# A gated dilated convolution on one Trainium2 core: matmuls reordered around waits, a load held back, a warm-up on a constant

## The chip, the core and the metric

The kernel runs on one core of a Trainium2 chip. The core has engines that work side by side, each through its own list of instructions in order: TensorE (matmuls; PE in the profile, with its weight loads as PEld), VectorE (DVE), ScalarE (ACT), GpSimd (POOL) and SyncE (SP), which here issues nearly all DMAs. They wait for one another by semaphores. Operands lie in SBUF, and matmul results in PSUM, whose banks hold 128 x 512 float32 each. The metric is device time in microseconds (us), the median of several runs.

## The reference

The input x has 2 sequences of 16000 steps with 256 channels, in bfloat16. A causal convolution with three taps at distance 2 makes 512 channels; the first half goes through tanh, the second through a sigmoid, the two are multiplied, and a 256 x 256 matrix projects the product.

```python
pad = (K - 1) * dil                      # K = 3, dil = 2
xp = jnp.pad(x, ((0, 0), (pad, 0), (0, 0)))
h = jnp.einsum('btc,cd->btd', xp[:, pad:pad + T, :], w[0])
for i in range(1, K):
    off = pad - i * dil
    h = h + jnp.einsum('btc,cd->btd', xp[:, off:off + T, :], w[i])
f = h[..., :D].copy()
g = h[..., D:].copy()
z = jnp.tanh(f) * _sigmoid(g)
return z @ w_o
```

## The kernel before

**Tiling.** The 32000 steps are cut into group 0 (512 steps), an extra group (512), an end group (256) and 15 wide groups of 2048. x is brought in with channels on partitions by transposing DMAs from SP (`load_plain` for the extra group, tile `xte`; `load_wide`, tile `xq`, two buffers; `load_end`, tile `xe`). Group 0 alone is loaded plainly (tile `osb`) and transposed on TensorE. Each group has four blocks, one for 128 of the 512 convolution channels, in the order tanh, sigmoid, tanh, sigmoid. Blocks are numbered through: 0 to 3 are group 0, 4 to 7 the first wide group, 8 to 11 the second, up to 63. The extra and end groups have blocks of their own.

**A wide block** does not apply the three taps one by one. VectorE first makes sums and differences of x at eight phases (tiles `q`, `qp`, `qm`, `qd`: `wide_pairs` L213, `wide_p` L219, `wide_m` L222, `wide_d` L231; GpSimd does quarters of `qd`). With weights combined at the start (`wmh`, `wph`, `wm`, `wt`, `wu`, `wd0`, `wd2`), TensorE then runs 14 matmuls of 512 columns into one two-bank PSUM tile `y` (three buffers):

- `first`, two with `wmh` on `qp` (L254); ScalarE copies the bank to `st` (`keep_first`, L276);
- `second`, two with `wph` on `qm` (L246); ScalarE copies the bank to `sv` (L280), and GpSimd makes the second half of `sv` (`other`, L283);
- `third`, two with `wm` on the other half of `qm`; then VectorE's `split_bank` (L286) forms the second bank of `y`;
- `late(0)`, four with `wt` and `wu` into both banks, which must follow `split_bank`; then VectorE's `rest` (L290) forms `sv`, which must read the banks before
- `late(1)`, four with `wd2` and `wd0`, goes on in them. ScalarE's activations read `sv` (L332) and `y` (L334).

Blocks of group 0, the extra and the end group apply the taps directly (`direct`, L310), in the order tap 2, tap 0, tap 1 (`TAPS`), two matmuls of 512 columns for tap 2 and tap 0 each, four of 256 for tap 1.

**Order.** Every engine's order is the program's order, written out by hand. Stage k of the main loop (k = 4 to 63), with V the block before and N the next, issues on TensorE: `late(V, 0)`, `second(B)`, any extra or end block, projections (`project`, L364, eight matmuls of 256 columns in the steady state), `first(N, 0)`, `third(B)`, `first(N, 1)`, `late(V, 1)`. Stage 5 has `second` and tap 0 of extra block 1 ahead of `late`. The extra blocks have their place in the early stages: block 0 ahead of the loop and in stage 4, block 1 in stages 4 and 5, block 2 in stage 6, block 3 in stage 7. Their PSUM tiles (`e_ps`) and those of the projection (`o_ps`) take turns in two buffers. VectorE's sums for later groups are filed under stages in the lists `small`, `big` and `mid`; `mid` holds one step only, `wide_m(G, 1)` of the second wide group, in stage 7, which runs right behind `rest(V)`. A gate (L339) multiplies the activations.

**Start.** VectorE sets a tile `warm` to zero, and 14 matmuls of 256 columns on it (L140) keep TensorE busy until x is there. SP's list begins with x of group 0, a weight, and then three transposing loads, the first wide group, the extra group and the second wide group. The third wide group's load takes the first one's buffer. ScalarE copies two halves of `wt` out of PSUM (`make_wt`, L436), and VectorE makes `wu` (L439).

**End.** Behind the loop, `late(V, 0)` of the last block, two projection pieces, `late(V, 1)`, four more pieces of the third pair (`left`), and the last eight pieces. Pieces go from PSUM to an `osb` tile (`out_evict` L401, `last_evict` L648) and are stored; `out_evict` stores two at a time (L381).

Of the kernel before, what the change touches and what calls it, by code (L numbers as in the profile page):

```python
# [13 lines left out]
def kernel(  # L14
# [23 lines left out]
    nc = tc.nc  # L38
    bf16 = mybir.dt.bfloat16
# [49 lines left out]
        return ps_y.tile([P, 2, BANK], f32, name="y")  # L89


    def load_end():

        xe = end["x"] = xt_pool.tile([P, 8, CT, RE], bf16, name="xe")
        rows = x[end["b"], 4 * (end["r0"] - 1):4 * (end["r0"] + RE), :].rearrange("(r j) c -> r (j c)", j=4)
        src = bass.AP(tensor=rows.tensor, offset=rows.offset, ap=[[4 * D, RE], [1, 8 * D]])
        nc.sync.dma_start_transpose(out=xe[:].rearrange("p j ct r -> p (j ct) r"), in_=src)
# [9 lines left out]
            in_=x[b, 4 * (r0 - RH):4 * (r0 + R), :].rearrange("(r j) c -> r (j c)", j=4),  # L107
        )

    def load_wide(n):  # L110
        G = wides[n]
        xq = G["x"] = xq_pool.tile([P, 8, CT, XW], bf16, name="xq")
        col, row = 0, 0
        G["cols"] = []
        for b, t0, rows in G["parts"]:
            lo = RH if t0 else 0
            if not t0:
                nc.gpsimd.memset(xq[:, :, :, col + RH - 1:col + RH], 0.0)
            nc.sync.dma_start_transpose(
                out=xq[:, :, :, col + RH - lo:col + RH + rows].rearrange("p j ct r -> p (j ct) r"),  # L120
                in_=x[b, t0 - 8 * lo:t0 + 8 * rows, :].rearrange("(r j) c -> r (j c)", j=8),
            )
            G["cols"].append((col + RH, slice(row, row + rows)))
            col, row = col + RH + rows, row + rows

    warm = consts.tile([P, BANK], bf16)
    nc.vector.memset(warm[:], 0.0)
    w_taps = [consts.tile([P, CT, D2], bf16, name=f"w{k}_sb") for k in range(K)]
    wo_sb = consts.tile([P, NT, D], bf16)
    xn = osb_pool.tile([P, 4, D], bf16, name="osb")  # L130
# [3 lines left out]
        nc.scalar.dma_start(out=w_taps[k][:], in_=w_in[k])  # L134
    nc.scalar.preload_act_table(ACT.Sigmoid)
    nc.sync.dma_start(out=w_taps[TAPS[1]][:], in_=w_in[TAPS[1]])
    for n in range(14):
        if n < 6 and n % 2 == 0:
            wps = new_y()
        nc.tensor.matmul(  # L140
            wps[:, 1, (n % 2) * 256:(n % 2 + 1) * 256], lhsT=warm[:, :P], rhs=warm[:, :256],
            start=n % 2 == 0 and n < 6, stop=True, skip_group_check=True,
        )
# [2 lines left out]
    load_plain(groups[0])  # L146
    load_wide(0)
    load_plain(extra)
    load_wide(1)
    loaded_wide = 2  # L150


    W = {nm: consts.tile([P, CT, D2], bf16, name=nm + "_sb") for nm in ("wd0", "wd2", "wph", "wmh", "wm", "wt", "wu")}
    ws_sb = consts.tile([P, CT, D2], f32)
    twos = [consts.tile([P, P], bf16, name=nm) for nm in ("plus2", "minus2")]

    def after(ins, behind):
        if behind is not None:
            tc.add_manual_dep(
                ins.ins, behind.ins.name,  # L160
                mybir.DependencyInfo(mybir.DependencyClass.Sync, mybir.DependencyReason.DATA),
                reason="GpSimd reads SBUF behind VectorE's instructions with two SBUF inputs",
            )
        return ins

    def weight_mm():

# [94 lines left out]
    def third(B):  # L262
        mm(B, W["wm"], B.G["qm"][:, 1], 0)
# [91 lines left out]
            return G["z"][:, dt, WIDE_PLACE[jp], lo:lo + P]  # L355
        return G["z"][:, dt, 2 * jp + q, rb0:rb0 + P]

    def out_mm(G, rb0, jp, o_ps=None):
        if o_ps is None:
            o_ps = ps_o.tile([P, 2, D], f32, name="o_ps", tag="o_ps")  # L360
        G["o", rb0, jp] = o_ps
        for q in range(2):
            for dt in range(NT):
                nc.tensor.matmul(  # L364
                    o_ps[q] if isinstance(o_ps, list) else o_ps[:, q, :], lhsT=z_columns(G, rb0, jp, q, dt), rhs=wo_sb[:, dt, :],
                    start=(dt == 0), stop=(dt == NT - 1),
                )
# [16 lines left out]
                )  # L384
            row += rows

    def out_evict(G, rb0, jp, on_dve):
        o_ps = G["o", rb0, jp]
        copy = nc.vector.tensor_copy if on_dve else nc.scalar.copy
        if jp is None:  # L390
            te = 4 * G["r0"]
            osb = consts.tile([P, 2, D], bf16, name="osb_end")
            copy(out=osb[:], in_=o_ps)
            rows = out[G["b"], te:te + 4 * RE, :].rearrange("(r q h) d -> h r q d", q=2, h=2)
            for h in range(2):
                nc.sync.dma_start(out=rows[h], in_=osb[h * RE:(h + 1) * RE])
            return
        h = jp % 2
        if h == 0:
            G["osb"] = osb_pool.tile([P, 4, D], bf16, name="osb")  # L400
        copy(out=G["osb"][:, 2 * h:2 * h + 2, :], in_=o_ps)  # L401
        if h == 1:
            store(G, rb0, slice(2 * jp - 2, 2 * jp + 2), G["osb"])


# [27 lines left out]
    nc.scalar.mul(W["wd2"][:], w_taps[2][:], 4.0)  # L433

    def make_wt(ct):
        nc.scalar.copy(out=W["wt"][:, ct, :], in_=W["y", ct][:])  # L436

    def make_wu(ct):
        nc.vector.scalar_tensor_tensor(  # L439
# [3 lines left out]
    make_wu(0)  # L443
    make_wt(1)
    make_wu(1)
    make_wt(0)
    for k in range(ND):
        direct(blocks[k], TAPS[2:], bank(blocks[k], k))
    for k in range(2):
# [9 lines left out]
    def extra_block(i, taps):  # L459
        E = extras[i]  # L460
        if TAPS[0] in taps:
            E.y = ps_o.tile([P, BANK], f32, name="e_ps", tag="o_ps")
        direct(E, taps, E.y[:])
        if TAPS[-1] in taps:
            activate(E, E.y[:])

    def plain_ends(func, i):
# [5 lines left out]
        dst = end["sg" if i else "th"]  # L473
        nc.scalar.activation(out=dst[:].rearrange("p h j r -> p (h j r)"), in_=ye[:], func=func, scale=1.0)

    for B in blocks[ND:ND + 2]:
        for ct in range(CT):
            first(B, ct)
        keep_first(B)
    extra_block(0, TAPS[:2])  # L480


    ready, todo, made = [], [], []
# [45 lines left out]
    for k in range(ND, NB):  # L529
        B, V = blocks[k], (blocks[k - 1] if k > ND else None)  # L530

        E = {
            ND: [(0, TAPS[2:]), (1, TAPS[:1])], ND + 1: [(1, TAPS[2:])], ND + 2: [(2, TAPS)],
            ND + 3: [(3, TAPS)],
        }.get(k, [])
        early_second = k == ND + 1
        if early_second:
            second(B)
            keep_second(B)
            extra_block(1, TAPS[1:2])  # L540
        if V:
            late(V, 0)
        if k >= ND + 2:
            Y = blocks[k - 2]
            activate(Y, "y")
            note_gates(Y, k)
        last = do(small, k) or last

        if k == ND + 6:
            todo.append(ready.pop())  # L550
        big_late = k == ND + 1

        def big_and_quarter(last):
            last = do(big, k) or last
            if B.oi == 0 and k > ND:
                quarter(B.G, 3, last)
            elif B.oi and not big_late and B.G["n"] + 1 < len(wides):
                for i in range(0 if k == ND + 2 else B.oi - 1, B.oi):
                    quarter(wides[B.G["n"] + 1], i, last)
            return last  # L560

        if not big_late:
            last = big_and_quarter(last)
        if not early_second:
            second(B)
            keep_second(B)
        if k == ND:
            for i in range(2, ND):
                activate(blocks[i], bank(blocks[i], i))
        other(B, last)  # L570
        if V:
            rest(V)
        last = do(mid, k) or last
        for e in E:
            extra_block(*e)
        if k in (ND + 4, ND + 5):
            plain_ends(*((ACT.Sigmoid, 1) if k == ND + 5 else (ACT.Tanh, 0)))

        project(0 if k < ND + 3 else 1 if k < ND + 6 else 2)
        evict()  # L580
        N = blocks[k + 1] if ND < k < NB - 1 else None

        split_first = k >= ND + 2
        if N:
            first(N, 0)
            if not split_first:
                first(N, 1)
        third(B)
        split_bank(B)
        if k == ND + 3:  # L590
            last = gates_of(extra, slice(0, 2))
        if big_late:
            last = big_and_quarter(last)
        if V:
            activate(V, "sv")
        if N:
            if split_first:
                first(N, 1)
            keep_first(N)
        if V:  # L600
# [11 lines left out]

    Y, V = blocks[NB - 2:]
    G = V.G
    late(V, 0)
    activate(Y, "y")
    big.pop(NB)
# [86 lines left out]
```

## Time and profile before

| | us |
|---|---|
| median of 3 runs | 263.51 (263.49 to 263.56) |
| profiled execution | 263.43 |
| its span, first to last instruction | 261.6 |
| TensorE busy | 256.0 |
| ScalarE busy | 245.9 |
| VectorE busy | 226.7 |
| GpSimd busy | 112.8 |

The profile is of one execution. The times of its rows count from the span's start; what lies around the span (263.43 against 261.6) is not told apart. A row of the timeline gives start, duration, engine, line, operation, tiles written and read, the shapes, and how many like instructions are merged in it; the bracket gives idle time ahead of it and what ended that. A row such as "SPq" or "ACTq" is a DMA being issued, not the transfer. Matmuls overlap, so a record is longer than the step from one to the next, and a row of n of them is as long as n steps and the overhang of the last. A row of the DMA issues gives the size and the median time from issue to landing. A row of the table by stage gives the stretch, its length, the busy time and number of instructions of each engine, the clock, the DMA share and the rate.

### The profile page before, as it was taken

Reading aid. Unit: us, or ns where it says so; the run is one execution under the profiler, and the core shown is the slowest. Engines: PE = TensorE matmul, PEld = TensorE weight load, DVE = VectorE, ACT = ScalarE, POOL = GpSimd, SP = SyncE. Lnnn points to the kernel's source line nnn. Section 1 sums busy time; section 2 is a strip of 40 time slices with the busy share of each in tenths; the row PEclk is TensorE's granted clock in tenths of the full one; section 3 lists DMA queues with packets and bytes.
Section 4 is the critical chain, followed back from the end, with each engine's and each line's share of the span. In section 5 each row is a group of like instructions: output and inputs, shape, how many; then the busy total and the mean of one; then the engine's idle time right before and its main releaser. Section 6 shows DMA issues by size and latency. Waiting matters only on the chain.

```text
span 261.6 us, 4231 instructions
## 1 busy us (share of the span) xinstructions
PE 256.0 (98%) x1464; PEld 144.2 (55%) x1464; DVE 226.7 (87%) x264; ACT 245.9 (94%) x378; POOL 112.8 (43%) x129
## 2 busy tenths in 40 slices
PE   8999999999999999999999999999999999999993
PEld 6644555555555555555555555555555555555562
DVE  2989969989889989999988988988988988986673
ACT  4668789999999999999999999999999999999993
POOL 1033434454453454355455355355345345444240
PEclk9999999999999999999999999999999999999998
DMA  7979073292834719256392934729274491221226
GB/s 209 201 177 192 0 180 94 83 209 83 175 119 123 209 52 212 111 117 174 96 175 105 199 120 103 203 79 215 81 169 124 101 231 43 80 83 40 82 80 241
DMA packets 79109, 35.10 MB, mean 134 GB/s; under 512 B 69232, under 2 KB 71536, under 8 KB 79088
## 3 DMA queue, kind: packets, MB, share of 16 engines
q1 hardware_dynamic: 77984, 33.92, 52.8%
q10 hardware_dynamic: 1104, 0.92, 1.1%
q8 instruction: 11, 0.18, 0.3%
q14 instruction: 10, 0.08, 0.1%
HBM read 1.18 MB, written 16.38 MB: 67 GB/s over the span
## 4 chain that ended last, share of the span: by engine, by line
PE 93%; DVE 3%; issue 1%; DMA 1%; ACT 0%; DVEq 0%; ACTq 0%
PE y L246 58%; PE o_ps L364 19%; PE y L254 9%; PE y L310 2%; PE y L140 1%; PE e_ps L310 1%; PE f_ps L310 1%; DVE sv L290 1%; DVE y L286 1%; DMA out_dram<-osb 1%; DVE qm L222 1%; PE wt_ps L171 0%; ACT osb L401 0%; PE y L364 0%; DVE osb L648 0%
## 5 line engine op out<-in xcount | busy, mean ns | idle before, releaser
L283 POOL TENSOR_TENSOR sv<-sv,st 128x512 f32<-128x512 f32 x60 | 76.4, 1274 | 23.9 <-ACT sv L280 22.2
L231 POOL TENSOR_TENSOR qd<-xq 128x256 bf16<-128x256 bf16 (+2 forms) x60 | 34.9, 585 | 114.2 <-DVE zw L339 55.4
L290 DVE TENSOR_TENSOR sv<-sv,y 128x1024 f32<-128x1024 f32 x60 | 72.7, 1212 | 3.8 <-PE y L246 3.7
L246 PE MATMUL y<-qd,wd_sb 128*128 128x512 bf16 x240 | 61.6, 379 | 0.1
L401 ACT CAST osb<-o_ps 128x512 bf16<-128x512 f32 x114 | 61.1, 591 | 0.2 <-PE o_ps L364 0.2
L286 DVE SCALAR_TENSOR_TENSOR y<-st,y 128x512 f32<-128x512 f32 x60 | 41.8, 696 | 21.9 <-PE y L246 19.6
L364 PE MATMUL o_ps<-wo_sb,zw 128*128 128x256 bf16 x450 | 58.4, 273 | 0.0
L364 PEld LDWEIGHTS <-zw 128*128 128x128 bf16 x480 | 47.0, 98 | 17.1
L254 PE MATMUL y<-qp,wmh_sb 128*128 128x512 bf16 x120 | 44.8, 379 | 0.0
L246 PEld LDWEIGHTS <-wd_sb 128*128 128x128 bf16 x240 | 23.5, 98 | 28.5 <-issue 0.6
L280 ACT ACTIVATE sv<-y 128x512 f32<-128x512 f32 x60 | 35.9, 598 | 1.4 <-PE y L246 1.1
L213 DVE TENSOR_TENSOR q<-xq 128x2048 bf16<-128x2048 bf16 (+2 forms) x32 | 36.8, 1155 | 0.0
L276 ACT ACTIVATE st<-y 128x512 f32<-128x512 f32 x60 | 36.3, 607 | 0.2 <-PE y L254 0.2
L246 PE MATMUL y<-q,wt_sb 128*128 128x512 bf16 x120 | 35.7, 379 | 0.2 <-DVE y L286 0.2
L246 PE MATMUL y<-qm,wph_sb 128*128 128x512 bf16 x120 | 35.7, 379 | 0.0
L246 PE MATMUL y<-qm,wm_sb 128*128 128x512 bf16 x120 | 35.7, 379 | 0.0
L246 PE MATMUL y<-q,wu_sb 128*128 128x512 bf16 x120 | 35.7, 379 | 0.0
L339 DVE TENSOR_TENSOR zw<-thw,sgw 128x2048 bf16<-128x2048 bf16 x28 | 34.1, 1217 | 0.0
L332 ACT ACTIVATE thw<-sv 128x1024 bf16<-128x1024 f32 x30 | 32.4, 1078 | 0.4 <-DVE sv L290 0.4
L332 ACT ACTIVATE sgw<-sv 128x1024 bf16<-128x1024 f32 x30 | 32.4, 1078 | 0.0
L334 ACT ACTIVATE sgw<-y 128x1024 bf16<-128x1024 f32 x30 | 31.3, 1043 | 0.1
L334 ACT ACTIVATE thw<-y 128x1024 bf16<-128x1024 f32 x30 | 31.3, 1044 | 0.0
(68 smaller groups left out, 178.8 us busy)
## 6 DMA issues: line engine op xcount, KB each, us to landing
out_dram<-osb SPq DMA_DIRECT2D x56, 256.0 KB, 2.1
out_dram<-osb SPq DMA_DIRECT2D x6, 128.0 KB, 2.2
w_sb<-in_w_dram ACTq DMA_DIRECT2D x2, 256.0 KB, 4.4
out_dram<-osb SPq DMA_DIRECT2D x2, 160.0 KB, 2.0
osb<-in_x_dram SPq DMA_DIRECT2D x1, 256.0 KB, 3.2
w_sb<-in_w_dram SPq DMA_DIRECT2D x1, 256.0 KB, 4.3
xq<-in_x_dram SPq DMA_TRANSPOSE x16, 7.2
out_dram<-osb ACTq DMA_DIRECT2D x2, 128.0 KB, 2.2
```

Of the source, the lines that this page charges most:

```text
L213: ins = nc.vector.tensor_tensor(out=sums(G, "q")[:, h, :, :, :, sl].rearrange("p h q ct r -> p h (q ct) r"), in0=s, in1=a, op=ALU.subtract ...
L246: nc.tensor.matmul(B.y[:, bank, :], lhsT=wmat[:, ct, B.osl], rhs=mv[:, :, ct, :], start=False, stop=ct == CT - 1, skip_group_check=True,)
L254: nc.tensor.matmul(B.y[:, 0, :], lhsT=W["wmh"][:, ct, B.osl], rhs=B.G["qp"][:, :, ct, :], start=ct == 0, stop=ct == CT - 1, skip_group_che ...
L276: nc.scalar.mul(B.st[:], B.y[:, 0, :], 4.0)
L280: nc.scalar.mul(B.sv[:, 0], B.y[:, 0, :], 2.0)
L283: after(nc.gpsimd.tensor_tensor(out=B.sv[:, 1], in0=B.sv[:, 0], in1=B.st[:], op=ALU.subtract), behind)
L286: nc.vector.scalar_tensor_tensor(out=B.y[:, 1, :], in0=B.st[:], scalar=-0.5, in1=B.y[:, 0, :], op0=ALU.mult, op1=ALU.add)
L290: nc.vector.tensor_tensor(out=B.sv[:], in0=B.sv[:], in1=B.y[:], op=ALU.subtract)
L332: nc.scalar.activation(out=dst[:, 2:4, :], in_=B.sv[:], func=func, scale=0.25)
L334: nc.scalar.activation(out=dst[:, 0:2, :], in_=B.y[:], func=func, scale=0.25)
L364: nc.tensor.matmul(o_ps[q] if isinstance(o_ps, list) else o_ps[:, q, :], lhsT=z_columns(G, rb0, jp, q, dt), rhs=wo_sb[:, dt, :], start=(dt ...
L401: copy(out=G["osb"][:, 2 * h:2 * h + 2, :], in_=o_ps)
```

## The change

Eight edits, in the order of the program:

- The warm-up's operand is a constant of ones that is read with a zero step instead of a tile that VectorE sets; there are 15 matmuls instead of 14.
- The second wide group's load is issued behind the second copy of `make_wt`, by an added dependency of SP on ScalarE. It stays the fourth DMA of x in SP's list. (`after`, which adds the dependency, is moved up and takes a reason.)
- Tap 2 of extra block 0 goes ahead of `first` of blocks 4 and 5; tap 0 stays behind them.
- In stage 5, the first matmul of `first` of block 6 goes ahead of `late` of block 4.
- Tap 2 of extra block 2 goes from stage 6 to stage 5, behind `third` of block 5; tap 2 of extra block 3 goes from stage 7 to the end of stage 6's extra work.
- In stage 7, the step in `mid` goes from behind `rest(V)` to behind `split_bank(B)`.
- Behind the loop, the first half of the next projection piece goes ahead of `late(V, 0)` of the last block, its second half to where the piece was.
- The four pieces `left` are stored one by one.

```diff
-    def load_wide(n):
+    def load_wide(n, behind=None):
...
-            nc.sync.dma_start_transpose(
+            load = nc.sync.dma_start_transpose(
...
+            after(load, behind, "the start of a transposing load holds up the end of the one before it")
...
-    warm = consts.tile([P, BANK], bf16)
-    nc.vector.memset(warm[:], 0.0)
+    warm = nc.const_aps.tensor(1.0, [P, BANK], bf16)
...
-    for n in range(14):
+    for n in range(15):
...
     load_plain(extra)
-    load_wide(1)
     loaded_wide = 2
...
-    def out_mm(G, rb0, jp, o_ps=None):
+    def out_mm(G, rb0, jp, o_ps=None, qs=(0, 1)):
...
-        for q in range(2):
+        for q in qs:
...
-        if h == 1:
+        if single:
+            store(G, rb0, slice(2 * jp, 2 * jp + 2), G["osb"][:, 2 * h:2 * h + 2])
+        elif h == 1:
             store(G, rb0, slice(2 * jp - 2, 2 * jp + 2), G["osb"])
...
-    make_wt(0)
+    load_wide(1, make_wt(0))
...
+    extra_block(0, TAPS[:1])
     for B in blocks[ND:ND + 2]:
         for ct in range(CT):
             first(B, ct)
         keep_first(B)
-    extra_block(0, TAPS[:2])
+    extra_block(0, TAPS[1:2])
...
-            ND: [(0, TAPS[2:]), (1, TAPS[:1])], ND + 1: [(1, TAPS[2:])], ND + 2: [(2, TAPS)],
-            ND + 3: [(3, TAPS)],
+            ND: [(0, TAPS[2:]), (1, TAPS[:1])], ND + 1: [(1, TAPS[2:])], ND + 2: [(2, TAPS[1:]), (3, TAPS[:1])],
+            ND + 3: [(3, TAPS[1:])],
...
             extra_block(1, TAPS[1:2])
+            first(blocks[k + 1], 0)
         if V:
             late(V, 0)
...
             rest(V)
-        last = do(mid, k) or last
         for e in E:
             extra_block(*e)
...
         if N:
-            first(N, 0)
+            if not early_second:
+                first(N, 0)
             if not split_first:
                 first(N, 1)
         third(B)
+        if early_second:
+            extra_block(2, TAPS[:1])
         split_bank(B)
+        last = do(mid, k) or last
...
+    half = todo[0]
+    out_mm(*half, None, (0,))
     late(V, 0)
...
     gate_phases(0, slice(2, 4))
-    project(2)
+    out_mm(*half, half[0]["o", half[1], half[2]], (1,))
+    made.append(todo.pop(0))
+    project(1)
     evict()
...
-    out_evict(*left[0][0], True)
+    out_evict(*left[0][0], True, True)
...
-    out_evict(*left[0][1], True)
+    out_evict(*left[0][1], True, True)
...
-    out_evict(*left[1][0], False)
-    out_evict(*left[1][1], False)
+    out_evict(*left[1][0], False, True)
+    out_evict(*left[1][1], False, True)
```

More of the change, by code (lines that the diff above doesn't have):

```diff
@@ L89, in new_y, with after @@
         return ps_y.tile([P, 2, BANK], f32, name="y")
+    def after(ins, behind, why="GpSimd reads SBUF behind VectorE's instructions with two SBUF inputs"):
+        if behind is not None:
+            tc.add_manual_dep(
+                ins.ins, behind.ins.name,
+                mybir.DependencyInfo(mybir.DependencyClass.Sync, mybir.DependencyReason.DATA),
+                reason=why,
+            )
+        return ins
     def load_end():
@@ L155 @@
     twos = [consts.tile([P, P], bf16, name=nm) for nm in ("plus2", "minus2")]
[L157 to L164, printed above, removed]
     def weight_mm():
@@ L385, in store, with out_evict @@
             row += rows
-    def out_evict(G, rb0, jp, on_dve):
+    def out_evict(G, rb0, jp, on_dve, single=False):
         o_ps = G["o", rb0, jp]
@@ L435, in make_wt @@
     def make_wt(ct):
-        nc.scalar.copy(out=W["wt"][:, ct, :], in_=W["y", ct][:])
+        return nc.scalar.copy(out=W["wt"][:, ct, :], in_=W["y", ct][:])
     def make_wu(ct):
```

## The prediction

> **What bounds the kernel now.** I read the page's head for the span, then the table by stage, then the timeline of both ends, because the table leaves no room in the middle.
>
> ```profile
> span 261.6 us, 4231 instructions
> ```
>
> ```profile
> 48.00:244.00 196.00, 196.00 (x1111) 108.53 (x1110) 177.75 (x202) 196.00 (x303) 93.23 (x104) 1.00 0.53 131
> ```
>
> TensorE is the bound: busy for 196.00 of 196.00 us from 48 to 244 (the first column behind the width). The change leaves the order of work in that stretch as it is. What can be won lies ahead of 48 us and behind 244 us, in gaps between matmuls. Their records overlap, so a gap shows as a distance of starts beyond the normal step:
>
> ```profile
> 16.31 0.69 DVE L286 SCALAR_TENSOR_TENSOR y<-st,y 128x512 f32<-128x512 f32 x1 [0.81 <-PE y L246]
> 16.48 0.59 PE L310 MATMUL e_ps<-xte,w_sb 128*128 128x512 bf16 x2
> 17.06 0.59 PE L246 MATMUL y<-q,wt_sb 128*128 128x512 bf16 x2
> 17.49 0.59 PE L246 MATMUL y<-q,wu_sb 128*128 128x512 bf16 x2
> 18.19 1.22 DVE L290 TENSOR_TENSOR sv<-sv,y 128x1024 f32<-128x1024 f32 x1
> 18.79 0.59 PE L246 MATMUL y<-qm,wm_sb 128*128 128x512 bf16 x2
> 19.47 1.02 PE L246 MATMUL y<-qd,wd_sb 128*128 128x512 bf16 x4
> ...
> 27.29 1.27 POOL L283 TENSOR_TENSOR sv<-sv,st 128x512 f32<-128x512 f32 x1
> 27.69 1.42 DVE L222 TENSOR_TENSOR qm<-q 128x1024 bf16<-128x1024 bf16 x1
> 27.91 0.59 PE L246 MATMUL y<-qm,wm_sb 128*128 128x512 bf16 x2
> 29.03 0.68 DVE L286 SCALAR_TENSOR_TENSOR y<-st,y 128x512 f32<-128x512 f32 x1
> 29.76 0.59 PE L246 MATMUL y<-q,wt_sb 128*128 128x512 bf16 x2 [0.17 <-DVE y L286]
> ```
>
> From wt to wu two 512-column matmuls step 17.49 - 17.06 = 0.43, so 0.216 each; a 256-column one takes half, 0.11. *Gap 1:* 16.48 + 0.43 = 16.91, but wt starts at 17.06: 0.15, waiting for the bank that VectorE (L286, block 4) leaves at 17.00. *Gap 2:* 18.79 + 0.43 = 19.22 against 19.47: 0.24, waiting for L290 of block 4, done at 19.41. *Gap 3:* between the pair at 27.91 and wt at 29.76 stand `first` and four wd, seven matmuls in all: 27.91 + 7 x 0.216 = 29.42, so 0.33 is waiting, for L286 of block 7, which stood behind the 1.42 us sum L222. *Gap 4* is in the tail:
>
> ```profile
> 248.46 1.02 PE L246 MATMUL y<-qd,wd_sb 128*128 128x512 bf16 x4
> 249.48 0.59 PE L246 MATMUL y<-q,wt_sb 128*128 128x512 bf16 x2
> ```
>
> 248.46 + 0.86 = 249.32 against 249.48: 0.16. Together 0.88 us.
>
> **The change part by part.**
>
> *Gap 1.* One matmul of block 6 (0.216) now goes between tap 0 of extra block 1 and `late` of block 4. It covers 0.15. Its bank is freed by ScalarE's activations of blocks 2 and 3, which stand ahead of the stage's other ScalarE work; I take it as free. Gain 0.15; were the bank late, between that and nothing.
>
> *Gap 2.* `late` of block 4 now starts at 16.91 + 0.216 = 17.12, 0.06 later than before, so L290 ends 0.06 later, near 19.47. TensorE gets there after tap 2 of extra block 2 (two matmuls, 0.43), near 19.50. About 0.03 of the gap stays; gain 0.21. The 0.43 was pulled forward from the stage behind, which in turn takes tap 2 of extra block 3 from the stage of block 7. So that stage (k = 6) stands where it did, and the gain of gaps 1 and 2 is cashed only in the stage of block 7, which has two matmuls fewer.
>
> *Gap 3.* There both could be lost again: TensorE comes to `late` of block 7 0.4 earlier, while L286 could not start before L222 was through at 29.11. The change puts L222 behind L286. L286 is then bound by the pair of `third` of block 7, which moves from 27.91 to about 27.5:
>
> ```profile
> 31.36 1.21 DVE L290 TENSOR_TENSOR sv<-sv,y 128x1024 f32<-128x1024 f32 x1
> 33.02 0.59 PE L246 MATMUL y<-qm,wm_sb 128*128 128x512 bf16 x2
> 33.72 0.69 DVE L286 SCALAR_TENSOR_TENSOR y<-st,y 128x512 f32<-128x512 f32 x1 [1.15 <-ACT osb L401]
> ```
>
> One stage later, with nothing else in its way, L286 stands 33.72 - 33.02 = 0.7 behind its pair. So it starts near 28.22, with VectorE free since L222's old start at 27.69, and ends near 28.9; TensorE is ready at 27.52 + 1.51 = 29.03. No wait, gain 0.33, but with a margin of 0.1. What is late next is L222, and behind it two gates and L290 of block 7. The set L286, L222, gates, L290 ran from 27.69 to 32.57 with L222 at 1.42 beside GpSimd's L283 (27.29 to 28.56). Behind L286 that is over; the nearest undisturbed row of L222's form is L219 at 0.69 (11.74, below). The set then ends at 32.57 + 0.53 - 0.73 = 32.4, against `late` of block 7 at 33.02 + 0.65 - 0.73 = 32.94. Even at 1.42 it ends near 33.1, a wait of 0.2. The 1.15 of idle time ahead of 33.72 says that VectorE has room, and from there on the engines move with TensorE.
>
> *Start, warm-up, loads.*
>
> ```profile
> 0.74 0.40 SPq L132 DMA_DIRECT2D osb<-in_x_dram  x1
> 0.86 0.27 DVE L127 MEMSET warm<- 128x256 uint32 x1 [0.86 <-PEq L688]
> 1.19 3.17 PE L140 MATMUL y<-warm 128*128 128x256 bf16 x14 [1.19 <-DVE warm L127]
> 4.15 0.63 PE L183 MATMUL tp<-ident,osb 128*128 128x128 bf16 x4
> 7.96 1.36 SPq L105 DMA_TRANSPOSE xte<-in_x_dram  x1
> 9.26 1.23 ACT L436 CAST wt_sb<-wt_ps 128x512 bf16<-128x512 f32 x2 [0.77 <-PE wt_ps L171]
> 9.36 5.56 SPq L119 DMA_TRANSPOSE xq<-in_x_dram  x1
> 11.74 0.69 DVE L219 TENSOR_TENSOR qp<-q 128x1024 bf16<-128x1024 bf16 x1
> 12.55 1.05 PE L254 MATMUL y<-qp,wmh_sb 128*128 128x512 bf16 x4
> 17.63 4.41 SPq L119 DMA_TRANSPOSE xq<-in_x_dram  x1
> 20.03 1.22 DVE L213 TENSOR_TENSOR q<-xq 128x2048 bf16<-128x2048 bf16 x1
> ```
>
> ```profile
> xte<-in_x_dram SPq DMA_TRANSPOSE x1, 3.6
> xq<-in_x_dram SPq DMA_TRANSPOSE x1, 8.2
> ```
>
> ```profile
> osb<-in_x_dram SPq DMA_DIRECT2D x1, 256.0 KB, 3.2
> ```
>
> The warm-up no longer waits for VectorE's memset. SP's queue begins at 0.74 and VectorE at 0.86; I take 0.85 for TensorE. Fifteen matmuls at the 0.21 of this stretch ((4.15 - 1.19) / 14) end near 4.02, and x, issued at 0.74, lands 3.2 later, at 3.9. So the transposes start about 0.13 earlier. This is slow-clock time: work begun 0.13 earlier at half rate is worth 0.07 at the full rate that follows. The trace has no matmul on a broadcast constant. The ends: TensorE as early as 0.74, held by x at 3.9 (gain 0.12), and no earlier start with a fifteenth matmul on top (loss 0.1). I take a gain of 0.07, nearest to the rows of the other engines.
>
> Tap 2 of extra block 0 ahead of the first wide product permutes work: its x lands at 7.96 + 3.6 = 11.6 and is wanted near 12.5; the first product (12.55, wanting qp of 12.43) moves 0.43 back and has 0.43 less behind it. Zero. The second wide x is issued behind the copies L436 (9.26 + 1.23 = 10.49) instead of at 9.36; with its 8.2 it lands at 18.7, and L213 wants it at 20.03. Zero, hidden by 1.3 us of VectorE's other work; without that cover its lateness would go to TensorE. On SP only the load of 17.63 stands behind it, and 10.5 + 5.6 = 16.1 leaves SP free in time.
>
> *Tail.* Half a projection piece (two matmuls, 0.22) fills gap 4; `late` of the last block starts 0.06 later, all that follows it on TensorE 0.16 earlier.
>
> ```profile
> 253.04 0.69 DVE L620 TENSOR_TENSOR zw<-thw,sgw 128x1024 bf16<-128x1024 bf16 x1
> 253.15 1.02 ACT L334 ACTIVATE sgw<-y 128x1024 bf16<-128x1024 f32 x1
> 253.82 1.91 PE L364 MATMUL y<-wo_sb,zw 128*128 128x256 bf16 x16
> 255.66 1.42 DVE L648 CAST osb<-y 128x512 bf16<-128x512 f32 x2 [0.73 <-ACT osb L648]
> 255.66 3.02 SPq L649 DMA_DIRECT2D out_dram<-osb  x6
> ```
>
> The gate L620 ends at 253.73, where the 0.06 puts it slightly later, and the matmuls of 253.82 want it, so these keep 0.1 at most. But the end hangs on ScalarE's line: L334, its casts, VectorE's cast at 255.66, then stores that SP issues one behind the other, 3.02 / 6 = 0.5 each. L334 waits for TensorE alone and comes 0.16 earlier. Between 0 and 0.16 I take 0.12. The four single stores in place of two pairs cost SP two issues more, ahead of 255.66. One of them in the way of a later store would add its 0.5; bytes gone earlier may shorten the queue at the end by as much. Zero, since SP stands idle ahead of 255.66.
>
> Sum: 0.15 + 0.21 + 0.33 + 0.07 + 0.12 = 0.88. The profiled execution took 263.43 (the span and 1.8 around it), so 262.55; the median of the runs is 0.08 higher: 262.6.
>
> **Rivals.** *The wait is handed on.* If L286 of block 7 still ends near 29.7 because VectorE is late by another route, gaps 1 to 3 all come back there, and start and tail are left: 263.51 - 0.19 = 263.3. For it: margins of 0.1. Against it: VectorE is free from 27.69.
>
> *The clock rises earlier.*
>
> ```profile
> 5.12:6.98 1.86, 1.86 (x9) 1.32 (x10) 1.00 1.20 253
> 6.98:7.76 0.78, 0.78 (x9) 0.58 (x6) 1.00 1.27 290
> ```
>
> In these stretches of L310 (TensorE first) the step falls from 1.86 / 9 = 0.21 to about 0.1 at 6.98, though the clock column says 1.00 in both. If the longer warm-up brought the full rate before 4.15, TensorE would save some 1.3 (half of 6.98 - 4.15), but the first product needs qp at 12.43. With tap 2 ahead it starts at 12.5 instead of 12.9, so 0.4 more is won: 262.2. Against it: the 14 matmuls from 1.19 did not do it. [...]
>
> *The second wide x is late: slower.* The diff says that a transposing load's start holds up the end of the one before it. The load of 17.63 now starts 1.1 ahead of the landing at 18.7. If that landing waited for the later load's issue (17.63 + 4.41 = 22.04), L213 would start 2.0 late, and nearly all of it would reach TensorE by way of VectorE: 262.6 + 1.8 = 264.4. It decides from a landing some 1.5 past 20.03, where gain and loss are level. Against it: xte landed at 11.6 while the next load issued until 14.92.
>
> **Numbers.** A measurement tells 0.2%, 0.53 us, from no change: faster is below 262.98, slower above 264.04. Forecast 0.68 (own range 262.3 to 262.95); handed on, in part or whole, 0.15 (262.9 to 263.4); clock 0.06; late x 0.11, other losses of that sign in it. Faster: 0.68 and 0.06, and a little of the second: 0.76. Same: 0.13. Slower: 0.11. The range 262.1 to 263.35 takes in the clock and nearly all of the handed-on wait.
>
> **What would show it.** Right: wt of block 4 follows the matmul ahead by 0.22, wd of block 4 comes within 0.05 of the pair ahead, L286 of block 7 starts near 28.2 with L222 behind it at 0.69, and L286 of block 8 stands near 33.0. TensorE's first matmul stands near 0.85, the transposes near 4.02. Wrong: a gap ahead of wt of block 7, a first matmul near 1.2, or L213 of the second wide group after 20.1.

## The result and the profile after

| | before | after |
|---|---|---|
| median of 7 runs each | 263.51 us (263.25 to 263.92) | 262.68 us (262.47 to 262.90) |
| profiled execution | 263.43 | 262.82 |
| its span | 261.6 | 261.0 |

The ratio is 0.9966, with a 95% interval of 0.9956 to 0.9975: a gain of 0.8 us, near the forecast of 262.6. The two profiled executions stand only 0.61 apart. Where that came from, and where a part of it was lost again, is read by setting like rows side by side. In the changed kernel the lines named here carry numbers one lower (L245 for the matmuls of L246, L285 for L286, L289 for L290), and the warm-up is L149; the kernels of the experiments carry the one or the other.

The timeline of the changed kernel, from the start to the stage of block 8 (columns as before):

```profile
0.78 3.36 PE L149 MATMUL y<-const-bfloat16-1.0 128*128 128x256 bf16 x15 [0.78 <-PEq L698]
3.93 0.63 PE L182 MATMUL tp<-ident,osb 128*128 128x128 bf16 x4
4.90 2.22 PE L309 MATMUL y<-xt,w_sb 128*128 128x256 bf16 x16
...
10.76 1.23 DVE L212 TENSOR_TENSOR q<-xq 128x2048 bf16<-128x2048 bf16 x1 [0.31 <-DMA xq<-in_x_dram]
12.03 0.69 DVE L218 TENSOR_TENSOR qp<-q 128x1024 bf16<-128x1024 bf16 x1
12.78 0.39 PE L253 MATMUL y<-qp,wmh_sb 128*128 128x512 bf16 x1 [0.25 <-DVE qp L218]
...
15.95 1.28 POOL L282 TENSOR_TENSOR sv<-sv,st 128x512 f32<-128x512 f32 x1 [14.57 <-ACT th L335]
16.69 0.38 PE L253 MATMUL y<-qp,wmh_sb 128*128 128x512 bf16 x1
16.70 1.08 DVE L230 TENSOR_TENSOR qd<-xq 128x1024 bf16<-128x1024 bf16 x1
16.90 0.59 PE L245 MATMUL y<-q,wt_sb 128*128 128x512 bf16 x2
18.30 1.21 DVE L289 TENSOR_TENSOR sv<-sv,y 128x1024 f32<-128x1024 f32 x1
18.85 0.60 PE L309 MATMUL e_ps<-xte,w_sb 128*128 128x512 bf16 x2
19.56 0.59 PE L245 MATMUL y<-qd,wd_sb 128*128 128x512 bf16 x2
...
27.57 0.59 PE L245 MATMUL y<-qm,wm_sb 128*128 128x512 bf16 x2
28.27 0.70 DVE L285 SCALAR_TENSOR_TENSOR y<-st,y 128x512 f32<-128x512 f32 x1 [0.51 <-ACT osb L400]
28.88 0.69 DVE L221 TENSOR_TENSOR qm<-q 128x1024 bf16<-128x1024 bf16 x1
29.08 0.59 PE L245 MATMUL y<-q,wt_sb 128*128 128x512 bf16 x2
33.04 0.69 DVE L285 SCALAR_TENSOR_TENSOR y<-st,y 128x512 f32<-128x512 f32 x1 [0.61 <-ACT osb L400]
```

- **Start.** TensorE begins at 0.78 in place of 1.19, its transposes at 3.93 in place of 4.15. The 16 matmuls at 4.90 took 2.22 where the like row of before took 2.81: the step fell from 0.21 to 0.11 at about 5.5 in place of 6.98. But the first wide x, landing at 10.74 (10.19 in the profile of before), let VectorE begin only at 10.76 (10.48 before), so that `qp` came at 12.72 (12.43 before), and TensorE, early because its step had halved earlier, waited for it.
- **Gap 1** is closed: 16.69 + 0.216 = 16.906, and wt starts at 16.90.
- **Gap 2** is not: 18.85 + 0.43 = 19.28 against 19.56, 0.28. Still the place is better than before: wd at 19.47 then, 19.56 now with 0.43 more behind it, so 0.34 ahead.
- **Gap 3** is closed: 27.57 + 1.51 = 29.08, where wt starts; before it was at 29.76, so TensorE is 0.68 ahead.

In the middle, which the prediction held unchanged, something new stands. The timeline of the changed kernel near 209 us, and then of before:

```profile
208.59 0.59 PE L245 MATMUL y<-qm,wm_sb 128*128 128x512 bf16 x2
209.23 1.03 PE L245 MATMUL y<-qd,wd_sb 128*128 128x512 bf16 x4
209.66 0.69 DVE L285 SCALAR_TENSOR_TENSOR y<-st,y 128x512 f32<-128x512 f32 x1 [0.70 <-PE y L253]
210.41 0.38 PE L245 MATMUL y<-q,wt_sb 128*128 128x512 bf16 x1
```

```profile
209.26 0.59 PE L246 MATMUL y<-qm,wm_sb 128*128 128x512 bf16 x2
209.97 0.70 DVE L286 SCALAR_TENSOR_TENSOR y<-st,y 128x512 f32<-128x512 f32 x1 [0.34 <-PE y L246]
210.77 0.59 PE L246 MATMUL y<-q,wt_sb 128*128 128x512 bf16 x2
```

Up to here TensorE is 209.26 - 208.59 = 0.67 ahead. L286 starts 0.71 behind its pair before, 1.07 after, although nothing that it waits for is later: it lost 0.36, and wt comes at 210.41 where 209.23 + 0.86 = 210.09 was possible. At wt the lead is down to 210.77 - 210.41 = 0.36. The tail of the changed kernel:

```profile
248.09 1.02 PE L245 MATMUL y<-qd,wd_sb 128*128 128x512 bf16 x4
248.95 0.38 PE L363 MATMUL o_ps<-wo_sb,zw 128*128 128x256 bf16 x2
249.17 0.59 PE L245 MATMUL y<-q,wt_sb 128*128 128x512 bf16 x2
252.63 1.02 ACT L333 ACTIVATE sgw<-y 128x1024 bf16<-128x1024 f32 x1
255.14 1.42 DVE L658 CAST osb<-y 128x512 bf16<-128x512 f32 x2 [0.61 <-ACT osb L658]
```

Gap 4 is closed (248.95 + 0.22 = 249.17). ScalarE's last `y` activation is 253.15 - 252.63 = 0.52 earlier, VectorE's cast the same, and that is 0.15 more than the 0.37 with which `late` came in (248.46 - 248.09).

### The profile page after: what moved, and what is told of

It is laid out like the page before. It is cut to its first block, busy times and chain, and to the rows that moved or that the text cites. A ratio compares the mean times of both kernels' runs of the same rounds, so it can differ in the third digit from the quotient of the medians.

```text
span 261.0 us, 4236 instructions
## 1 busy us (share of the span) xinstructions
PE 255.7 (98%) x1465; PEld 143.8 (55%) x1465; DVE 225.9 (87%) x263; ACT 246.0 (94%) x378; POOL 112.9 (43%) x129
## 4 chain that ended last, share of the span: by engine, by line
PE 91%; DMA 3%; DVE 2%; issue 1%; SPq 0%; ACT 0%; DVEq 0%; ACTq 0%
PE y L245 59%; PE o_ps L363 19%; PE y L253 10%; DMA xq<-in_x_dram 3%; PE e_ps L309 1%; PE y L363 1%; PE f_ps L309 1%; DVE y L285 1%; DVE q L212 0%; DVE sv L289 0%; DVE qd L230 0%; DVE osb L658 0%; DVE qp L218 0%; ACT osb L658 0%; SPq L145 0%
## 5 line engine op out<-in xcount | busy, mean ns | idle before, releaser
L282 POOL TENSOR_TENSOR sv<-sv,st 128x512 f32<-128x512 f32 x60 | 76.5, 1274 | 24.0 <-ACT th L335 14.6
L230 POOL TENSOR_TENSOR qd<-xq 128x256 bf16<-128x256 bf16 (+2 forms) x60 | 34.9, 586 | 113.6 <-DVE zw L338 55.6
L289 DVE TENSOR_TENSOR sv<-sv,y 128x1024 f32<-128x1024 f32 x60 | 72.7, 1211 | 3.8 <-PE y L245 3.7
L245 PE MATMUL y<-qd,wd_sb 128*128 128x512 bf16 x240 | 61.6, 379 | 0.1
L285 DVE SCALAR_TENSOR_TENSOR y<-st,y 128x512 f32<-128x512 f32 x60 | 41.8, 696 | 21.9 <-PE y L245 18.8
L245 PEld LDWEIGHTS <-wd_sb 128*128 128x128 bf16 x240 | 23.5, 98 | 28.5 <-issue 0.6
L212 DVE TENSOR_TENSOR q<-xq 128x2048 bf16<-128x2048 bf16 (+2 forms) x32 | 36.8, 1155 | 0.3 <-DMA xq<-in_x_dram 0.3
L245 PE MATMUL y<-q,wt_sb 128*128 128x512 bf16 x120 | 35.7, 379 | 0.1
L245 PE MATMUL y<-qm,wph_sb 128*128 128x512 bf16 x120 | 35.7, 379 | 0.0
L245 PE MATMUL y<-q,wu_sb 128*128 128x512 bf16 x120 | 35.7, 379 | 0.0
L245 PE MATMUL y<-qm,wm_sb 128*128 128x512 bf16 x120 | 35.7, 379 | 0.0
```

Of the source, the lines that this page charges most:

```text
L212: ins = nc.vector.tensor_tensor(out=sums(G, "q")[:, h, :, :, :, sl].rearrange("p h q ct r -> p h (q ct) r"), in0=s, in1=a, op=ALU.subtract ...
L245: nc.tensor.matmul(B.y[:, bank, :], lhsT=wmat[:, ct, B.osl], rhs=mv[:, :, ct, :], start=False, stop=ct == CT - 1, skip_group_check=True,)
L282: after(nc.gpsimd.tensor_tensor(out=B.sv[:, 1], in0=B.sv[:, 0], in1=B.st[:], op=ALU.subtract), behind)
L285: nc.vector.scalar_tensor_tensor(out=B.y[:, 1, :], in0=B.st[:], scalar=-0.5, in1=B.y[:, 0, :], op0=ALU.mult, op1=ALU.add)
L289: nc.vector.tensor_tensor(out=B.sv[:], in0=B.sv[:], in1=B.y[:], op=ALU.subtract)
```

## The experiments

The runs were taken in three groups, each on one chip beside the kernel before; the medians of before were 263.56 (the first four experiments), 263.36 (the next four) and 263.52 (the last four). Medians of different groups are therefore compared to 0.1 or 0.2 at best.

**The loop's moves alone.** The kernel before with the reordered stages 5 to 7 and nothing else.

```diff
-            ND: ..., ND + 2: [(2, TAPS)], ND + 3: [(3, TAPS)],
+            ND: ..., ND + 2: [(2, TAPS[1:]), (3, TAPS[:1])], ND + 3: [(3, TAPS[1:])],
...
+            first(blocks[k + 1], 0)
         if V:
             late(V, 0)
...
+        if early_second:
+            extra_block(2, TAPS[:1])
         split_bank(B)
+        last = do(mid, k) or last
```

> The kernel before with the moves in stages 5 to 7 alone (first matmul of block 6, taps 2 of extra blocks 2 and 3, the sum L222 behind split_bank). Theory A (the gain is the closed gaps in the loop, plus smaller parts at both ends): gaps 1 and 3 close for 0.15 and 0.33, gap 2 for between 0 and 0.21, so 0.5 to 0.7 of the 0.83: 262.8 to 263.0. Rival B (the gain comes from the earlier start and an earlier rise of the clock, the moves alone only hand the wait on): within 0.15 of the kernel before, 263.4 to 263.6.

262.93 (262.55 to 263.21), ratio 0.9975 [0.9965, 0.9986]: 0.63 of the 0.8 us. In its profile gaps 1 to 3 are closed and gap 4 stays. Near 209 us it has no late L286.

**The sum L221 put back ahead of L285**, all else as changed.

```diff
             rest(V)
+        last = do(mid, k) or last
...
         split_bank(B)
-        last = do(mid, k) or last
```

> The changed kernel with the sum of stage 7 put back behind rest(V), ahead of split_bank. Theory A: split_bank of block 7 stands behind that sum again, near 29.0, and wt of block 7 starts near 29.7 instead of 29.08, so gaps 1 to 3 come back there in one wait of about 0.6: 263.2 to 263.3. Rival C (split_bank is bound by TensorE, the sum's place is of no account): 262.7, as the changed kernel.

263.26 (262.76 to 263.86), ratio 0.9987 [0.9978, 0.9995]. The timeline at gap 3:

```profile
27.67 1.27 POOL L282 TENSOR_TENSOR sv<-sv,st 128x512 f32<-128x512 f32 x1
28.07 1.42 DVE L221 TENSOR_TENSOR qm<-q 128x1024 bf16<-128x1024 bf16 x1
28.60 1.03 PE L245 MATMUL y<-qd,wd_sb 128*128 128x512 bf16 x4
29.41 0.68 DVE L285 SCALAR_TENSOR_TENSOR y<-st,y 128x512 f32<-128x512 f32 x1
30.15 0.59 PE L245 MATMUL y<-q,wt_sb 128*128 128x512 bf16 x2 [0.52 <-DVE y L285]
```

TensorE is ready at 28.60 + 0.86 = 29.46 and starts at 30.15: it gives back 0.69 in one place, what gaps 1 to 3 had won. (Ahead of this, TensorE had waited 1.35 for the extra x in this execution, the slowest of its kernel; that has no part in the 0.69.) By the medians 0.5 is given back, against 262.75 for the changed kernel in this group. So at this place the reordering of TensorE's list is worth nothing without that of VectorE's, which is the forecast's step for gap 3.

**The old warm-up**, all else as changed: VectorE zeroes a tile, and 14 matmuls read it.

```diff
-    warm = nc.const_aps.tensor(1.0, [P, BANK], bf16)
+    warm = consts.tile([P, BANK], bf16)
+    nc.vector.memset(warm[:], 0.0)
...
-    for n in range(15):
+    for n in range(14):
```

> The changed kernel with VectorE's zero tile and 14 warm-up matmuls again. Theory A: TensorE starts near 1.19 and loses 0.07 to 0.2: 262.75 to 262.9. Rival B (the start carries the gain): 263.2 or more. The profile is also to show whether the clock's rise (5.52 in the changed kernel, 6.97 before) belongs to the start: rise near 7.0 if it does, anywhere if it is chance.

262.46 (262.28 to 262.62), ratio 0.9954 [0.9942, 0.9967]: undoing a part made the kernel 0.2 to 0.3 faster, though its first matmul was at 1.19 again. Its profile has no late L286 near 209.

**The changed kernel once more**, for the spread between executions.

> The changed kernel once more, for its time beside the others of this call and for a second profile. Theory A: 262.5 to 262.9. If the 0.31 wait near 210 and the first wide x landing at 10.74 (before: 10.19) were chance of the one profiled execution, they are gone or elsewhere; if they belong to the change, they stand again at 209.9 and 10.7. With x at 10.2 gap 2 should be closed (wd of block 4 within 0.05 of the pair ahead), since GpSimd's L282 then starts before VectorE's L230 wants to run.

262.75 (262.53 to 263.04), ratio 0.9966 [0.9953, 0.9978]; gap 2 at 0.26, and the late L285 again.

**The second wide x not held.**

```diff
     load_plain(extra)
+    load_wide(1)
...
-    load_wide(1, make_wt(0))
+    make_wt(0)
```

> The changed kernel with the second wide x issued straight behind the extra group's x again. Theory H0 (the hold is of no account, as x of the extra group is not on the path): 262.75, as the changed kernel beside it in the last call, and the first wide x lands where it did there, 10.7. Theory H1 (the hold shortens the landing of the extra group's x): without it that x lands later, 12.0 to 12.9, TensorE waits for it ahead of extra block 0, and the time is 262.9 or more. Theory H2 (the hold itself lengthens the first wide x's load, 10.7 against 10.2 and 10.4 in the two kernels without it): it lands near 10.2 and the time falls to 262.5.

262.63 (262.04 to 263.04), ratio 0.9966 [0.9954, 0.9978]: no different. Its profiled execution shows what the hold does (the timeline, then a row of the DMA issues; the same row of the changed kernel says 3.3):

```profile
12.79 0.39 PE L310 MATMUL e_ps<-xte,w_sb 128*128 128x512 bf16 x1 [1.55 <-DMA xte<-in_x_dram]
```

```profile
xte<-in_x_dram SPq DMA_TRANSPOSE x1, 4.4
```

The extra x takes 1.1 longer, and TensorE waits 1.55 for it in that execution, but the runs don't tell it apart. The hold does not rule such a wait out: of the eleven profiles with it, ten have 3.3 or 3.4 in this row, and that of e2_no_mid has 4.6, with the wait of 1.35 named there. Nor does the hold make the first wide x late: that landed at 10.62 here and at 10.74 with the hold.

**The tail undone**: `project(2)` in one, the pieces of `left` stored in pairs.

```diff
-    half = todo[0]
-    out_mm(*half, None, (0,))
     late(V, 0)
...
-    out_mm(*half, half[0]["o", half[1], half[2]], (1,))
-    made.append(todo.pop(0))
-    project(1)
+    project(2)
...
-    out_evict(*left[0][0], True, True)
+    out_evict(*left[0][0], True)
```

> The changed kernel with the tail of the kernel before (whole projection pieces behind late of the last block, pairs stored together). If the tail's two edits are worth the 0.15 that TensorE's last start gained in the two profiles: 262.9. If it is hidden by the stores at the end: 262.75. The profile shows a gap of 0.16 ahead of wt of the last block.

262.94 (262.58 to 263.06), ratio 0.9978 [0.9968, 0.9988]: 0.2 to 0.3 slower than the two series of the changed kernel. By chance this execution also shows gap 2 as the forecast had it. Its timeline there, and in the tail:

```profile
15.57 1.27 POOL L282 TENSOR_TENSOR sv<-sv,st 128x512 f32<-128x512 f32 x1 [14.19 <-DVE qd L230]
16.65 0.75 DVE L230 TENSOR_TENSOR qd<-xq 128x1024 bf16<-128x1024 bf16 x1
17.99 1.22 DVE L289 TENSOR_TENSOR sv<-sv,y 128x1024 f32<-128x1024 f32 x1
18.80 0.60 PE L309 MATMUL e_ps<-xte,w_sb 128*128 128x512 bf16 x2
19.26 1.02 PE L245 MATMUL y<-qd,wd_sb 128*128 128x512 bf16 x4
...
247.78 1.02 PE L245 MATMUL y<-qd,wd_sb 128*128 128x512 bf16 x4
248.80 0.59 PE L245 MATMUL y<-q,wt_sb 128*128 128x512 bf16 x2
```

18.80 + 0.43 = 19.23 against 19.26: closed. The first wide x landed at 10.36 here and at 10.74 in the changed kernel's profile, and VectorE and GpSimd are earlier by about as much: GpSimd, which waits for VectorE's first half of `qd`, is through at 16.84 where it was 17.23; L230, which meets it, ends 0.38 earlier, and L289 starts 0.31 earlier. TensorE's pair is only 0.05 earlier (18.80 against 18.85). In the tail gap 4 is back: 247.78 + 0.86 = 248.64 against 248.80.

**A way to close gap 2, with the old warm-up**: the gate that stands between L231 and L290 in stage 5 goes behind `split_bank`.

```diff
-    small[ND + 1] = [lambda: wide_d(G0, 0, nc.vector), lambda: gates_of(groups[0], slice(0, 2))]
+    small[ND + 1] = [lambda: wide_d(G0, 0, nc.vector)]
+    mid[ND + 1] = [lambda: gates_of(groups[0], slice(0, 2))]
```

> The changed kernel with VectorE's zero tile and 14 warm-up matmuls, and group 0's gate (0.68 us of VectorE) moved behind split_bank of stage 5, so that L290 of block 4 comes 0.6 earlier. If gap 2 was left open by VectorE being late (the gate and a sum slowed beside GpSimd ahead of L290), it closes: 0.1 to 0.25 under the 262.46 of the kernel without this move, 262.2 to 262.35. If the gate only pushes the wait on to split_bank and the sums behind it, 262.45 or more.

263.14 (262.99 to 263.28), ratio 0.9988 [0.9979, 0.9997]: 0.7 slower than the 262.46 of the same kernel with the gate in its place. The timeline:

```profile
19.18 1.02 PE L246 MATMUL y<-qd,wd_sb 128*128 128x512 bf16 x4
19.64 0.68 DVE L339 TENSOR_TENSOR z<-th,sg 128x1024 bf16<-128x1024 bf16 x1
20.43 1.06 ACT L332 ACTIVATE thw<-sv 128x1024 bf16<-128x1024 f32 x1 [1.55 <-DVE z L339]
21.39 0.58 ACT L276 ACTIVATE st<-y 128x512 f32<-128x512 f32 x1
22.02 0.59 PE L246 MATMUL y<-qm,wph_sb 128*128 128x512 bf16 x2 [0.95 <-ACT st L276]
```

Gap 2 is gone, but ScalarE's activation waits for the late gate to free its buffer, the copy `st` behind it is late, and TensorE waits for that bank. The wait was handed on, and grew.

**One idle instruction on VectorE**, on top of the changed kernel: is the place near 209 us one in VectorE's list?

```diff
     warm = nc.const_aps.tensor(1.0, [P, BANK], bf16)
+    nc.vector.memset(consts.tile([P, 2], bf16, name="filler")[:], 0.0)
```

> The changed kernel with one tiny VectorE memset of a tile that nobody reads in the place of the old one; the warm-up stays on the constant, with 15 matmuls. Theory F (the wait of 0.3 near 210, in all three profiles of kernels that lack VectorE's first instruction and in none that has it, comes from the place of an instruction in VectorE's list): the wait is gone and the time falls to 262.45. Theory S (it comes from TensorE's earlier start or the fifteenth matmul): it stays, 262.75. If the early start is worth its 0.07, this kernel is 0.07 under the 262.46 of the kernel with the zero tile; if VectorE's chain absorbs it, level.

262.38 (262.17 to 262.56), ratio 0.9957 [0.9944, 0.9969]: a kernel with one instruction more is 0.3 faster than the two series without it. Its timeline at the place:

```profile
208.22 0.59 PE L246 MATMUL y<-qm,wm_sb 128*128 128x512 bf16 x2
208.86 1.03 PE L246 MATMUL y<-qd,wd_sb 128*128 128x512 bf16 x4
208.92 0.69 DVE L286 SCALAR_TENSOR_TENSOR y<-st,y 128x512 f32<-128x512 f32 x1 [0.33 <-PE y L246]
209.73 0.59 PE L246 MATMUL y<-q,wt_sb 128*128 128x512 bf16 x2
```

L286 is back at 0.70 behind its pair, and wt starts without a wait (208.86 + 0.86 = 209.72). With the old warm-up the kernel took 262.46; the difference of 0.08 is all that the runs show for the earlier first matmul, and they don't tell it from nothing.

**Two idle instructions.**

```diff
+    for i in range(2):
+        nc.vector.memset(consts.tile([P, 2], bf16, name=f"filler{i}")[:], 0.0)
```

> The changed kernel with two tiny VectorE memsets instead of one. If the wait near 210 comes from one fixed place in VectorE's list of instructions, which falls on split_bank of block 52 only with no filler, it is gone here too: 262.4. If it comes with an odd or even count or something else of the start, it is back: 262.7.

262.44 (262.39 to 262.49), ratio 0.9956 [0.9943, 0.9969], the same as with one.

**Gap 2 from GpSimd's side**, with the idle instruction: GpSimd's `other` of block 4 no longer waits for the first half of `qd`, only for the sums ahead of it.

```diff
+        sums_made = last
         last = do(small, k) or last
...
-        other(B, last)
+        other(B, sums_made if k == ND else last)
```

> The kernel with the filler (262.38), and GpSimd's subtraction of block 4 placed behind the sum qm instead of behind the difference qd that follows it on VectorE. In the profiles with gap 2 still open, that subtraction ran beside VectorE's second qd, which took 1.07 instead of 0.69 and pushed L290 of block 4 back. If that is what keeps gap 2 open when TensorE comes early, GpSimd starts near 15.3 instead of 15.6 to 15.9, the second qd takes 0.69 to 0.85, gap 2 falls from 0.26 to 0.1 or less, and the time is 262.2 to 262.3. If the meeting only moves to the first qd and delays split_bank by as much, gap 2 stays and the time is 262.4.

262.00 (261.64 to 262.45), ratio 0.9945 [0.9931, 0.9959], the fastest version of all. The timeline:

```profile
14.78 1.53 POOL L283 TENSOR_TENSOR sv<-sv,st 128x512 f32<-128x512 f32 x1 [13.39 <-ACT sv L280]
16.08 0.77 DVE L231 TENSOR_TENSOR qd<-xq 128x1024 bf16<-128x1024 bf16 x1
17.42 1.22 DVE L290 TENSOR_TENSOR sv<-sv,y 128x1024 f32<-128x1024 f32 x1
18.23 0.60 PE L310 MATMUL e_ps<-xte,w_sb 128*128 128x512 bf16 x2
18.69 0.81 PE L246 MATMUL y<-qd,wd_sb 128*128 128x512 bf16 x3
```

GpSimd is through at 16.31, early in the second L231, the sum takes 0.77, and gap 2 is 18.69 - 18.23 - 0.43 = 0.03. Its range and that of the kernel with the idle instruction alone overlap, so the 0.38 between their medians is not a firm size.

**Tap 2 of extra block 0 back behind the first wide products**, with the idle instruction.

```diff
-    extra_block(0, TAPS[:1])
     for B in blocks[ND:ND + 2]:
...
-    extra_block(0, TAPS[1:2])
+    extra_block(0, TAPS[:2])
```

> The kernel with the filler, with both taps of extra block 0 behind the first wide products again. My prediction had this edit at nothing. If TensorE comes to the first product ahead of qp in most executions (clock risen before 6), it now has nothing to do until then: the gap there grows by 0.43, and what the later wait of gap 2 does not absorb, some 0.15 to 0.4, is lost: 262.5 to 262.8. If VectorE's chain sets the pace up to block 4 anyway, 262.4.

262.65 (262.28 to 262.80), ratio 0.9960 [0.9947, 0.9973]. TensorE waited 0.79 for `qp` in its profile, and 0.33 in that of the kernel with tap 2 ahead and one idle instruction; the first wide x landed 0.35 apart in the two. Counted from VectorE's first sum of it, L286 of block 8 comes 22.47 later here and 22.28 with tap 2 ahead: 0.19. The medians are 0.27 apart, and their ranges overlap. With tap 2 ahead gap 2 stood open (18.49 + 0.43 = 18.92 against 19.19); here it is closed, as 19.27 + 0.43 = 19.70:

```profile
19.27 0.60 PE L310 MATMUL e_ps<-xte,w_sb 128*128 128x512 bf16 x2
19.73 1.02 PE L246 MATMUL y<-qd,wd_sb 128*128 128x512 bf16 x4
```

**The pieces of `left` stored in pairs**, with the idle instruction; the half piece stays.

```diff
-    out_evict(*left[0][0], True, True)
+    out_evict(*left[0][0], True)
...
```

> The kernel with the filler, with the four pieces stored in pairs again; half a piece still goes ahead of late of the last block. Undoing both tail edits cost about 0.2 to 0.25 by the medians. If the half piece carries it, 262.4 here; if the single stores let the last store land earlier, 262.5 to 262.6.

262.25 (262.13 to 262.57), ratio 0.9952 [0.9938, 0.9966]. The runs show nothing of the single stores. In the profiles the last landing is 3.41 behind the start of the last matmul here, and 3.43 with single stores; but the span ends 1.04 behind that landing here and 0.91 with them. So it is in all fourteen: 1.03 or 1.04 with pairs (four profiles), 0.90 or 0.91 with single stores (ten). By the traces single stores are thus worth 0.1; why the end is shorter is not shown.

## Why the prediction was right, point by point

**The total.** 262.6 was forecast and 262.68 came, but that it came so near was luck: the sum held two errors that cancelled, a loss that was in no term (0.3), and about as much gained beyond the terms. Without that loss the kernel takes 262.38 (one idle instruction) or 262.44 (two), 0.98 and 1.08 below before in their groups, 0.1 to 0.2 more than the 0.88 of the sum. The profiles show where. In thirteen of the fourteen VectorE's first sum of the first wide x (L213) starts within 0.03 of the landing of that x, which came anywhere from 10.12 to 10.84; in that of before it starts 0.29 behind it. Counted from this sum, the profiles fall in line (us; from block 8 to block 52 all take 172.35 or 172.36):

| | first sum to L286 of block 8 | L286 of block 52 to the last matmul's start | from there to the span's end |
|---|---|---|---|
| before | 23.23 | 51.14 | 4.43 |
| e1_loop_only | 22.46 | 51.14 | 4.43 |
| changed kernel | 22.28 | 51.29 | 4.35 |
| e10_dve_filler | 22.28 | 50.99 | 4.34 |
| e12_no_first_tap | 22.47 | 50.99 | 4.34 |
| e11_other_early | 22.03 | 50.98 | 4.35 |
| e13_no_single | 22.28 | 50.99 | 4.45 |

So the loop's moves are worth 0.77 here, tap 2 ahead 0.19, the half piece 0.15, the single stores 0.1, and the loss costs 0.3. The gap 2 that is left would be 0.25 more. Between the profiles of before and after these add up to 0.88, of which the first sum of the later execution, 0.28 further back, leaves the 0.61 that stands in the table of times.

**Gaps 1 to 3**, forecast 0.69: 0.63 by the loop's moves alone. Gap 1 was right. Gap 3 was right in place and size: L285 at 28.27 (forecast near 28.2), TensorE ready at 29.08 (29.03), L221 at 0.69, L285 of block 8 at 33.04 (near 33.0). **Gap 2 was mis-sized** in the profile of the changed kernel: 0.28 of waiting is left where 0.03 was forecast. L289 ended at 19.51, where 19.47 was said; the error is TensorE's arrival, 19.28 in place of 19.50. The sum took it that TensorE comes there later by the inserted matmul alone. But TensorE, early because its step had halved earlier, did tap 2 of extra block 0 while `qp` was still being made, and so had 0.43 less behind the first product. VectorE did not come forward with it: its second L230, begun while GpSimd's `other` ran, ended 0.55 behind that at 17.78 (1.08 us in place of 0.69); `other` waited for VectorE's first half of `qd`, and all of them for the first wide x. With tap 2 put back (e12_no_first_tap) the gap is closed; with it ahead, e11_other_early closes it by taking GpSimd out of the way. In e7_no_tail's profile it is closed because x landed earlier and TensorE did not come earlier with it. So the gain of 0.21 is there only where this chain is as early as TensorE.

**The start**, forecast 0.07: first matmul 0.78 (0.85), transposes 3.93 (4.02), and a gain that is not to be told from nothing. The step that failed is that TensorE could use the time: in the profile after it waits for `qp`, early or not. From VectorE's first sum to block 8 e3_no_start, with its first matmul at 1.19, takes 22.27, as the kernels with 0.77 do, and that sum waits for its x.

**Tap 2 of extra block 0**, forecast at zero as mere permutation: 0.19 by the profiles, and most of what was gained beyond the terms. The term assumed that `qp` (12.43 before) is there when TensorE comes (12.55). In most of the other profiles TensorE comes first, and two matmuls ahead shorten the wait by up to their 0.43, of which the reopened gap 2 takes back 0.24. The medians with and without put it at 0.27, with overlapping ranges, so its size by the runs is open. The forecast leaned on a profile in which the step halved at 6.97, the latest of all fourteen, and TensorE came late.

**The held load**, forecast at zero: no difference in the runs. The rival of a late second wide x did not occur: in the profile after that x landed at 19.19 (18.7 was said), while the later load was issued until 21.95, and its sum L212 ran at 20.03, with no idle time ahead.

**The tail**, forecast 0.12: 0.15 in the trace from the half piece, which was right. The single stores, forecast at zero, are worth 0.1 in the traces, behind the last landing, where the sum had nothing; the runs don't show it.

**The clock's earlier rise**, a rival at 262.2: the step halved at 5.52 in the profile after and at 6.97 in that of before, but over all fourteen profiles it did so anywhere from 3.43 to 6.97, at 6.78 with the old warm-up and 6.70 with the new. It changes from one execution to the next and is no effect of the change. The clock column says 1.00 on both sides of it in both kernels, so that a clock is behind the halving is not shown. (Half of 6.98 - 4.15 is 1.4, not 1.3; nothing hangs on it.) What TensorE won by it in the profile after went into the wait for `qp`, so that even there it did not bring the rival's 0.4.

**What no term held.** VectorE's L285 of block 53, near 209 us, starts 0.34 to 0.36 late in all five profiles that lack the memset at the head of VectorE's list (the changed kernel twice, e2_no_mid, e5_no_hold, e7_no_tail), and in none of the nine others. One or two idle instructions remove it. (The expectation of two idle instructions calls the place block 52; the row is the fiftieth L285, and block 4 has the first.) So taking away the warm tile's memset cost 0.3 us, some 200 us behind it: that is shown. Why VectorE stops at this place in its list is not.

## What to carry to other kernels

When the bound engine's list is reordered to fill a gap, check whether the engine that frees the bank is paced by a third one: gap 2 opened again as soon as TensorE came earlier, because VectorE's sum took 1.08 us beside GpSimd's in place of 0.69. A move of work ahead of a first product is not a permutation when the operand of that product may come after TensorE does. And when a change adds or drops a single instruction, compare the two traces over their whole length: here 0.3 of 1.1 us went in a stretch in which the order of work was untouched. Compare them from the landing that the first work waits for: it moved by 0.7 between executions here, nearly as much as the whole change is worth.

## What the hardware showed that was not expected

**A late start at a fixed place in a list.** VectorE stood idle for 0.70 us ahead of L285 of block 53, and for 0.33 with one instruction more in its list, with all that it waits for as early as before. What it stood idle for is not shown.

**VectorE beside GpSimd.** Two sums that started while GpSimd's ran ended the same time behind it: GpSimd's L282 ends at 17.23 and VectorE's L230 at 17.78 in the changed kernel; in e2_no_mid L282 ends at 28.94 and L221 at 29.49; 0.55 both times, and 1.08 or 1.42 us in place of 0.69. One that started 0.02 ahead of the end of GpSimd's took 0.69 (L231 at 16.92 in the profile of before). What makes the two longer is not shown.

**Loads issued in a row.** The extra x took 4.4 us from issue to landing with the next transposing load issued right behind, 3.3 with that held back; in before and in e1_loop_only, not held, it took 3.6 and 4.3. With it held back ten of eleven profiles have 3.3 or 3.4, but e2_no_mid's has 4.6. So holding goes with a shorter load in these profiles, and does not ensure it; more of the reason that the diff gives for it is not shown.
